# Attention with a bucketed bias, then a bilinear feed-forward: the bias loads, the order of the first four pairs, and where two feed-forward quanta and the fifth pair's transposes stand

## The chip, the cores and the metric

The kernel runs on one core of a Trainium2 chip. The metric is the time of one execution on the device in microseconds. Engines are named as in the profile: PE (TensorE's matmuls) with PEld (its weight loads), DVE (VectorE), ACT (ScalarE), POOL (GpSimd) and SP (SyncE), which here only issues DMAs. POOL issues DMAs too, and ACT can.

## The reference

Two stages. The first is attention over 8 batches and 8 heads with 576 positions and a head size of 64, with a bias that depends only on the distance of two positions, by 32 buckets:

```python
scores = scale * np.matmul(q, k.transpose(0, 1, 3, 2))
...
bias = bias_table[bucket]
scores = scores + bias.transpose(2, 0, 1)[None, :, :, :]
scores = scores - np.max(scores, axis=-1, keepdims=True)
attn = np.exp(scores)
attn = attn / (np.sum(attn, axis=-1, keepdims=True) + 1e-09)
return np.matmul(attn, v).astype(np.float32)
```

The second takes the result as x, 4608 tokens of 512, and computes `((x @ w_a) * (x @ w_b)) @ w_out` with an inner size of 1536. Inputs and output are float32; the kernel computes in bfloat16 with float32 sums.

## The kernel before

**Units of work.** Attention is done in 32 pairs, a pair being two heads of one batch; four pairs make a batch. A pair needs q and k transposed (head dimension on the partitions, tile `qkT`), six score tiles, each followed by an exponential on ACT (four wide ones of 128x1024 elements, two smaller ones, "scores rest"), multiplications with the band on DVE, ten "av" groups on PE that multiply with v and with a column of ones, and the division on DVE (`rc`, then `xg`). `emit_x` transposes the result into `xn`, the input of the feed-forward: in batch 0 on PE with a DVE copy, later by a DMA. The feed-forward is cut into 9 chunks of 512 tokens, each of 12 blocks. A block is two *quanta*: `pa` (four matmuls of 512 columns with w_a, then a copy `ha` on ACT) and `pb` (four with w_b, then the product `g` on DVE). After the blocks, `po` multiplies with w_out.

**The band.** All distances over 128 fall in the last bucket, so exp(bias) differs from a constant only near the diagonal; the constant cancels in the division. `emit_table` loads the 32-row table four times one under the other (`bt`), its last row on all partitions (`bl`), and a constant one-hot matrix (`oh`), takes the difference, its exponential, and makes `ebd`. `emit_band(k)`, k from 0 to 5, makes a sixth of the band with 16 small matmuls into one PSUM bank, which DVE copies to `E` (L189). `copy_band_tail` makes a shifted copy `Et` for the last score tile, on POOL (L197); pairs from the fifth on use it, while the first four do that multiplication in two halves of 64 partitions (L297).

**Order.** The schedule is written out by hand: each engine does its instructions in the order in which the Python code emits them. The first four pairs (batch 0) have a loop of their own, without feed-forward work beside them. In it the av groups of one pair stand among the scores of the next. After it come the last pair's av groups, its x, two quanta, the fifth pair's transposes (L237, `emit_transposes_first(4, ring=True)`), and two more quanta. From the fifth pair on, a pair is 9 steps and a quantum stands in most of them.

**PSUM.** Of eight banks, four serve the scores in turn (two tiles of two banks, pool `pst`), and four (`m0` to `m3`) are given out in turn by `bank`: two for "av" (band, warm matmuls, av groups, x) and two for "ffn" (transposes, later the quanta). After the first four pairs av has one bank and ffn three. A matmul into a bank waits until the reader of the bank's earlier content is done.

**Queues.** POOL issues the loads of q, k, v and the weights in one queue, and each load waits there for the eighth load before it to land. `set_v` are the memsets of v's tile (a column of ones, and zeros in the last block of rows), also on POOL. SP issues the bias loads and, much later, the stores and the transposing DMAs. `emit_warm(n)` issues n matmuls of zeros with 512 columns.

Of the kernel before, what the change touches and what calls it, by code (L numbers as in the profile page):

```python
# [13 lines left out]
def kernel(  # L14
# [11 lines left out]
    nc = tc.nc  # L26
# [8 lines left out]
    NB = 32  # L35
# [133 lines left out]
    def emit_table():  # L169
        for g in range(4):  # L170
            nc.sync.dma_start(out=bt_sb[32 * g:32 * g + 32, :], in_=bias_table)
        nc.sync.dma_start(out=bl_sb[:, :],
                          in_=bias_table[NB - 1:NB, :].to_broadcast([128, H]))
        nc.sync.dma_start(out=oh_sb[:, :], in_=oh_handle.ap())
        nc.vector.tensor_tensor(out=bt_sb[:, :], in0=bt_sb[:, :], in1=bl_sb[:, :], op=SUB)
        nc.scalar.activation(out=eb_sb[:, :], in_=bt_sb[:, :], func=ACTF.Exp)
        nc.vector.tensor_tensor(
            out=ebd_sb[:, :, :],
            in0=eb_sb[:, :].rearrange("b (a h) -> b a h", a=1).to_broadcast([128, 4, H]),
            in1=oh_sb[:, 512:544].rearrange("b (a h) -> b a h", a=4), op=MULT)  # L180

    def emit_band(k):

        ps = bank("av", [128, 64, H], FP32, f"E{k}")
        for j in range(16):
            s = 380 - 4 * (16 * k + j)
            nc.tensor.matmul(out=ps[:, 4 * j:4 * j + 4, :], lhsT=oh_sb[:, s:s + 128],  # L187
                             rhs=ebd_sb[:, :, :], start=True, stop=True)
        nc.vector.tensor_copy(out=E_sb[:, :, 64 * k:64 * k + 64],  # L189
                              in_=ps[:, :, :].rearrange("p c h -> p h c"))  # L190

    def copy_band_tail():

        for hh in range(2):

            r, c0 = slice(64 * hh, 64 * hh + 64), 64 * hh
            nc.gpsimd.tensor_copy(out=Et_sb[r, :, :], in_=E_sb[r, hh::2, c0:c0 + 192])  # L197
# [9 lines left out]
    def emit_transposes(p):  # L207
# [7 lines left out]
        ps = pst.tile([128, 2, 1024], BF16, tag="st", name=f"tr{p}")  # L215
        for which in range(2):
            for j in range(LJ):
                nc.tensor.transpose(ps[:, which, LP * j:LP * j + LP],
                                    qk_tiles[b][2][:, hp, which, j, :], ident[0:LP, 0:LP])
        nc.scalar.activation(  # L220
# [3 lines left out]
    def emit_transposes_first(p, k_act=False, ring=False):  # L224
# [5 lines left out]
        for which, t in enumerate(qk_tiles[b][0:2]):  # L230
# [17 lines left out]
            else:  # L248
                nc.vector.tensor_copy(out=o, in_=i)

# [85 lines left out]
    def emit_x(p):  # L336
# [9 lines left out]
        for jq in range(5):  # L346
            nc.tensor.transpose(ps[:, jq, :], xg_of[p][:, jq, :], ident[:, :])
        nc.vector.tensor_copy(out=xn[:, hp, S * b:S * b + S],  # L348
                              in_=ps[:, :, :].rearrange("p j t -> p (j t)")[:, 0:S])
# [5 lines left out]
    def ffn_quanta(c):  # L355
        g = wrk.tile([128, NDF, 512], BF16, tag="g", name=f"g{c}")
        for df in range(NDF):
# [28 lines left out]
    def all_quanta():  # L386
        for c in range(NCH):
            yield from ffn_quanta(c)

    quanta = all_quanta()  # L390


# [25 lines left out]
    set_v(0, nc.gpsimd)  # L418
    load_v(0, 0, 4)
    load_v_tail(0)  # L420
    load_qk(0, 4, 8)
# [3 lines left out]

    emit_transposes_first(0)
    emit_band(0)
    emit_tails(0)

# [5 lines left out]
    for p in range(4):  # L435
# [8 lines left out]
        else:  # L444
            emit_band(1)
            emit_band(2)
        emit_scores(p, 2)
        if p:
            emit_avs(p - 1, 0 if p == 1 else 4, 4 if p == 1 else 6)
        else:  # L450
            emit_band(3)
            emit_band(4)
        emit_scores(p, 3)
        if p < 3:
            emit_transposes_first(p + 1, k_act=(p == 1))
        if p:
            emit_avs(p - 1, 4 if p == 1 else 6, 10)
        else:
            emit_band(5)
# [3 lines left out]
        emit_scores_rest(p)  # L463
        if p == 0:
# [4 lines left out]
            copy_band_tail()  # L469
# [7 lines left out]
    emit_x(2)  # L477
    emit_avs(3, 0, 10)
    emit_x(3)
    banks.update(av=(0,), ffn=(2, 3, 1))  # L480
    next(quanta)
    next(quanta)
    emit_transposes_first(4, ring=True)
# [16 lines left out]
    for p in range(4, NP + 1):  # L500
# [7 lines left out]
        for s in range(9):  # L508
# [19 lines left out]
            if s == (4 if p == 5 else 1) and p + 1 < P_DMA:  # L528
                emit_transposes(p + 1)
# [62 lines left out]
```

## Time and profile before

| | us |
|---|---|
| median of 3 runs (419.4, 419.59, 420.15) | 419.59 |
| the profiled execution | 420.81 |
| its span, from the first to the last instruction | 419.0 |
| busy PE / DVE / ACT / POOL | 404.1 / 238.1 / 230.8 / 80.6 |
| first band matmul starts | 8.50 |
| first wide exponential starts | 9.82 |
| first scores of the second, third, fourth, fifth pair start | 15.70 / 21.53 / 26.86 / 40.71 |

Times inside a profile count from the span's start. The time of a run is longer than the span by what lies before and after the instructions, 1.81 us in the profiled execution. A line of the profile names the line of the kernel, the engine, the operation, the tile written and the tiles read; "idle" is the time for which the engine stood before that instruction, with the event that ended it. "Pair 0" is the first pair and "pair 4" the fifth, as in the names of the tiles; words ("the fifth pair") count from one.

### The profile page before, as it was taken

What the parts mean: (1) busy time and instruction counts of PE and PEld (TensorE: products, weight loads), DVE (VectorE), ACT (ScalarE), POOL (GpSimd) and SP (SyncE); (2) the same over time, 40 slices, a digit from 0 to 9 for tenths busy, and PEclk for the clock granted to TensorE, in tenths of its full rate; (3) what the DMA queues carried; (4) which work ended last, traced back from release to release, by engine and by line L of the source; (5) the groups of instructions that cost most, each with busy time, mean ns of one, the idle gap of its engine ahead of it and who ended that gap; (6) DMA issues with size and microseconds to landing.
All of it is one profiled execution on the core that took longest, in us unless ns stands there. A gap on an engine that the chain in (4) does not pass through costs nothing.

```text
span 419.0 us, 8668 instructions
## 1 busy us (share of the span) xinstructions
PE 404.1 (96%) x3488; PEld 208.0 (50%) x3488; DVE 238.1 (57%) x574; ACT 230.8 (55%) x313; POOL 80.6 (19%) x138
## 2 busy tenths in 40 slices
PE   5979999999999999999999999999999999999996
PEld 2655455545555555555555555454554554444442
DVE  3896666666565755576556656665546553332431
ACT  2993888556655666466646674567556631321320
POOL 8874531113111211103011311130000000000000
PEclk8899999999999999999999999999999999999999
DMA  9999994689759685968698978983242012002002
GB/s 97 159 208 188 200 140 57 138 173 182 104 94 207 115 100 109 199 107 125 97 167 150 131 102 148 180 126 53 70 119 45 17 40 94 1 2 100 2 0 100
DMA packets 109449, 46.60 MB, mean 111 GB/s; under 512 B 84576, under 2 KB 104800, under 8 KB 109408
## 3 DMA queue, kind: packets, MB, share of 16 engines
q0 software_dynamic: 54304, 18.88, 40.6%
q1 hardware_dynamic: 55104, 27.16, 26.4%
q8 instruction: 27, 0.44, 0.4%
q14 instruction: 14, 0.11, 0.1%
HBM read 37.90 MB, written 15.93 MB: 128 GB/s over the span
## 4 chain that ended last, share of the span: by engine, by line
PE 87%; DMA 3%; DVE 3%; ACT 3%; issue 1%; SPq 1%; DVEq 0%; ACTq 0%
PE pb L368 22%; PE pa L360 22%; PE po L377 21%; PE av L322 8%; PE st L266 7%; PE av L319 2%; ACT at L268 2%; DMA qk_scratch<-qkn 2%; PE st L284 2%; PE st L276 2%; DMA oh_sb<-oh_const 1%; DVE at L302 1%; DMA xn<-xg 1%; PE E L187 1%; DVE xg L332 1%
## 5 line engine op out<-in xcount | busy, mean ns | idle before, releaser
L268 ACT ACTIVATE at<-st 128x1024 bf16<-128x1024 f32 x128 | 123.9, 1022 | 51.5 <-PE st L266 50.9
L371 DVE TENSOR_TENSOR g<-pb,ha 128x512 bf16<-128x512 f32 x108 | 74.6, 691 | 76.2 <-PE pb L368 52.2
L364 ACT ACTIVATE ha<-pa 128x512 f32<-128x512 f32 x108 | 64.7, 599 | 92.8 <-PE pa L360 92.8
L360 PE MATMUL pa<-xn,wa 128*128 128x512 bf16 x432 | 111.2, 379 | 0.5 <-DMA xn<-xg 0.5
L368 PE MATMUL pb<-xn,wb 128*128 128x512 bf16 x432 | 111.0, 379 | 0.0
L377 PE MATMUL po<-wo,g 128*128 128x512 bf16 x432 | 101.7, 379 | 0.0
L322 PE MATMUL av<-vb,at 128*128 128x65 bf16 x1280 | 64.4, 194 | 0.0
L302 DVE TENSOR_TENSOR at<-at,E 128x768 bf16<-128x768 bf16 (+2 forms) x128 | 61.6, 501 | 4.6 <-ACT at L268 3.7
L377 PEld LDWEIGHTS <-g 128*128 128x128 bf16 x432 | 39.6, 98 | 49.0 <-issue 7.9
L322 PEld LDWEIGHTS <-at 128*128 128x128 bf16 x1280 | 55.4, 98 | 16.3 <-issue 1.5
L368 PEld LDWEIGHTS <-wb 128*128 128x128 bf16 x432 | 38.7, 97 | 46.4 <-issue 7.8
L360 PEld LDWEIGHTS <-wa 128*128 128x128 bf16 x432 | 38.5, 98 | 43.2 <-issue 7.0
L381 DVE COPY ob<-po 128x512 f32<-128x512 f32 x36 | 24.9, 692 | 52.5 <-PE po L377 52.4
L266 PE MATMUL st<-qkT 64*128 64x512 bf16 x256 | 41.3, 389 | 2.9 <-ACT at L279 1.2
L498 POOL COPY pace<-at 1x1 bf16<-1x1 bf16 x22 | 4.2, 192 | 179.4 <-DVE at L302 179.4
L319 PE MATMUL av<-vb,at 128*128 128x130 bf16 x160 | 35.5, 222 | 2.0 <-DVE xn L348 1.5
L332 DVE TENSOR_TENSOR xg<-av,rc 128x384 bf16<-128x384 f32 x64 | 31.4, 491 | 2.2
L279 ACT ACTIVATE at<-st 128x512 bf16<-128x512 f32 x32 | 19.2, 599 | 23.1 <-PE st L276 23.1
L133 POOL DMA_DIRECT2D vb<-in_v_dram x36 | 30.7, 864 | 5.9 <-PE pb L368 2.5
L330 DVE RECIPROCAL rc<-av 128x6 f32<-128x6 f32 x64 | 11.8, 185 | 27.8 <-PE av L322 27.8
L319 PEld LDWEIGHTS <-at 128*128 128x128 bf16 x160 | 15.6, 98 | 16.9 <-issue 2.3
L286 ACT ACTIVATE at<-st 128x576 bf16<-128x576 f32 x32 | 20.7, 647 | 0.0
(53 smaller groups left out, 184.4 us busy)
## 6 DMA issues: line engine op xcount, KB each, us to landing
out_dram<-ob SPq DMA_DIRECT2D x36, 256.0 KB, 2.4
qk_scratch<-qkn SPq DMA_DIRECT2D x22, 288.0 KB, 3.8
ql<-in_q_dram POOLq DMA_DIRECT2D x15, 288.0 KB, 5.5
kl<-in_k_dram POOLq DMA_DIRECT2D x15, 288.0 KB, 6.5
vb<-in_v_dram POOLq DMA_DIRECT2D x28, 128.0 KB, 6.4
wa<-in_moe_w_a_dram POOLq DMA_DIRECT2D x4, 384.0 KB, 10.2
wb<-in_moe_w_b_dram POOLq DMA_DIRECT2D x4, 384.0 KB, 11.0
wo<-in_moe_w_out_dram POOLq DMA_DIRECT2D x4, 384.0 KB, 8.0
```

The source lines that it names most:

```text
L133: nc.gpsimd.dma_start(out=vb2[b % 2][:, h0:h1, i, 0:Dh], in_=v[b, h0:h1, 128 * i:128 * i + 128, :].transpose([1, 0, 2]))
L266: nc.tensor.matmul(out=st[:, hh, :], lhsT=kT[r, 128 * i:128 * i + 128], rhs=qT[r, 0:512], start=True, stop=True)
L268: nc.scalar.activation(out=at[:, 2 * i:2 * i + 2, 0:512], in_=st[:, :, :], func=ACTF.Exp, scale=scale)
L302: nc.vector.tensor_tensor(out=at[:, sl, q0:q0 + w], in0=at[:, sl, q0:q0 + w], in1=e, op=MULT)
L319: nc.tensor.matmul(out=pav[:, j, :, :], lhsT=at[:, 8, 128 * jq:128 * jq + 128], rhs=vb[:, 2 * hp:2 * hp + 2, 4, :], start=True, stop=False)
L322: nc.tensor.matmul(out=pav[:, j, hh, :], lhsT=at[:, 2 * i + hh, 128 * jq:128 * jq + 128], rhs=vb[:, 2 * hp + hh, i, :], start=False, stop= ...
L332: nc.vector.tensor_tensor(out=xo.rearrange("p j (h d) -> p j h d", h=2), in0=pav[:, :, :, 0:Dh], in1=rc[:, 0:n, :, :].to_broadcast([128, n ...
L360: nc.tensor.matmul(out=ps[:, :], lhsT=wa_sb[:, mc, 128 * df:128 * df + 128], rhs=xn[:, mc, 512 * c:512 * c + 512], start=(mc == 0), stop=( ...
L364: nc.scalar.activation(out=ha[:, :], in_=ps[:, :], func=ACTF.Copy)
L368: nc.tensor.matmul(out=ps[:, :], lhsT=wb_sb[:, mc, 128 * df:128 * df + 128], rhs=xn[:, mc, 512 * c:512 * c + 512], start=(mc == 0), stop=( ...
L371: nc.vector.tensor_tensor(out=g[:, df, :], in0=ps[:, :], in1=ha[:, :], op=MULT)
L377: nc.tensor.matmul(out=ps[:, :], lhsT=g[:, df, 128 * tt:128 * tt + 128], rhs=wo_sb[:, df, :], start=(df == 0), stop=(df == NDF - 1))
```

## The change

1. *Bias loads.* `bt` is loaded with one broadcasting DMA instead of four, and `bt` and `bl` are issued by ACT; SP only issues `oh`. A one-element Exp, on data that is there at once, stands ahead of the table's exponential on ACT.
2. *Start of pair 0.* Bands 0 and 1 come ahead of pair 0's transposes, and band 2 right behind them. The transposes go into four quarter tiles (two of them in the scores' banks), copied by ACT and DVE, two each. ACT copies band 1.
3. *First four pairs.* The other bands move up by one place; pair 0's av groups all come behind pair 2's transposes (six of them) and behind pair 1's last scores (four). Warm matmuls: six are added, in pairs 0 and 1.
4. *Tail of the band.* It is copied by ACT instead of POOL, after the fourth pair's scores.
5. *Hand-over.* x2 is copied by ACT. The first two quanta (block 0 of chunk 0) are cut into four parts by the four slices of x; parts 0 and 1 come ahead of the fourth pair's av groups, parts 2 and 3 behind its x. The fifth pair's transposes come ahead of the fourth pair's x.
6. *Pair 5* (the sixth): its transposes use two ffn banks instead of a score tile, and are copied by ACT (q) and DVE (k).
7. *POOL's queue.* v's first loads come ahead of the memsets of v's tile, which in the built program then wait for these loads to land, and the load of q and k for heads 4 to 7 is cut in two.

```diff
     def emit_table():
-        for g in range(4):
-            nc.sync.dma_start(out=bt_sb[32 * g:32 * g + 32, :], in_=bias_table)
-        nc.sync.dma_start(out=bl_sb[:, :],
-                          in_=bias_table[NB - 1:NB, :].to_broadcast([128, H]))
+        nc.scalar.dma_start(out=bt_sb[:, :], in_=bias_table.rearrange("(g b) h -> g b h", g=1)
+                            .to_broadcast([4, NB, H]))
+        nc.scalar.dma_start(out=bl_sb[:, :],
+                            in_=bias_table[NB - 1:NB, :].to_broadcast([128, H]))
         nc.sync.dma_start(out=oh_sb[:, :], in_=oh_handle.ap())
+        nc.scalar.activation(out=pace_sb[:, :], in_=warm[0:1, 0:1], func=ACTF.Exp)
...
-    def emit_band(k):
+    def emit_band(k, act=False):
...
+        if act:
+            nc.scalar.activation(out=o, in_=i, func=ACTF.Copy)
+        else:
+            nc.vector.tensor_copy(out=o, in_=i)
...
-            nc.gpsimd.tensor_copy(out=Et_sb[r, :, :], in_=E_sb[r, hh::2, c0:c0 + 192])
+            nc.scalar.activation(out=Et_sb[r, :, :], in_=E_sb[r, hh::2, c0:c0 + 192], func=ACTF.Copy)
...
-    def emit_transposes(p):
+    def emit_transposes(p, ring=True):
...
+            p_ = ps[:, which, :] if ring else bank("ffn", [128, 1024], BF16, f"tr{p}_{which}")[:, :]
...
+    def emit_transposes_pair0():
+
+        qkT = wrk.tile([128, 2, S], BF16, tag="qkT", bufs=3, name="qkT0")
+        qkT_of[0], qT_of[0], kT_of[0] = qkT, qkT[:, 0, :], qkT[:, 1, :]
+        for which, t in enumerate(qk_tiles[0][0:2]):
+            o = qkT[:, which, :].rearrange("c (p j) -> c p j", j=LJ)
+            for half in range(2):
+                if which == 0:
+                    ps = bank("ffn", [128, 3, LP], BF16, f"tr0_0_{half}")
+                else:
+                    ps = pst.tile([128, 3, LP], BF16, tag="st", name=f"tr0_1_{half}")
+                for j in range(3):
+                    for hh in range(2):
+                        c0 = Dh * (3 * half + j)
+                        nc.tensor.transpose(ps[64 * hh:64 * hh + 64, j, :], t[:, hh, c0:c0 + Dh],
+                                            ident[0:LP, 0:LP])
+                o_ = o[:, :, 3 * half:3 * half + 3]
+                i_ = ps[:, :, :].rearrange("c j p -> c p j")
+                if half == 0:
+                    nc.scalar.activation(out=o_, in_=i_, func=ACTF.Copy)
+                else:
+                    nc.vector.tensor_copy(out=o_, in_=i_)
...
+    class EarlyQuanta:
+
+
+        def __init__(self):
+            self.g = wrk.tile([128, NDF, 512], BF16, tag="g", name="g0")
+            self.ps = [ffn_bank(f"{n}0_0") for n in ("pa", "pb")]
+
+        def part(self, mc):
+            for ps, w_sb in zip(self.ps, (wa_sb, wb_sb)):
+                nc.tensor.matmul(out=ps[:, :], lhsT=w_sb[:, mc, 0:128], rhs=xn[:, mc, 0:512],
+                                 start=(mc == 0), stop=(mc == NMC - 1))
+            if mc == NMC - 1:
+                ha = wrk.tile([128, 512], FP32, tag="ha", name="ha0_0")
+                nc.scalar.activation(out=ha[:, :], in_=self.ps[0][:, :], func=ACTF.Copy)
+                nc.vector.tensor_tensor(out=self.g[:, 0, :], in0=self.ps[1][:, :], in1=ha[:, :],
+                                        op=MULT)
...
     load_qk(0, 2, 4)
-    set_v(0, nc.gpsimd)
     load_v(0, 0, 4)
     load_v_tail(0)
-    load_qk(0, 4, 8)
+    set_v(0, nc.gpsimd)
+    load_qk(0, 4, 6)
+    load_qk(0, 6, 8)
     load_v(0, 4, 8)
     load_w_in(0)
     load_qk(1, 0, 4)
 
-    emit_transposes_first(0)
     emit_band(0)
+    emit_band(1, act=True)
+    emit_transposes_pair0()
+    emit_band(2)
     emit_tails(0)
...
         else:
-            emit_band(1)
-            emit_band(2)
-        emit_scores(p, 2)
-        if p:
-            emit_avs(p - 1, 0 if p == 1 else 4, 4 if p == 1 else 6)
-        else:
             emit_band(3)
             emit_band(4)
+        emit_scores(p, 2)
+        if p > 1:
+            emit_avs(p - 1, 4, 6)
+        elif p:
+            emit_warm(3)
+        else:
+            emit_band(5)
+            emit_warm(1)
         emit_scores(p, 3)
         if p < 3:
             emit_transposes_first(p + 1, k_act=(p == 1))
         if p:
-            emit_avs(p - 1, 4 if p == 1 else 6, 10)
+            emit_avs(p - 1, 0 if p == 1 else 6, 6 if p == 1 else 10)
         else:
-            emit_band(5)
+            emit_warm(2)
             emit_mult(0, 0)
             emit_mult(0, 1)
         emit_mult(p, 2)
         emit_scores_rest(p)
+        if p == 1:
+            emit_avs(0, 6, 10)
...
-            copy_band_tail()
...
-    emit_x(2)
+    emit_x(2, act=True)
+    copy_band_tail()
+    early = EarlyQuanta()
+    early.part(0)
+    early.part(1)
     emit_avs(3, 0, 10)
+    emit_transposes_first(4, ring=True)
     emit_x(3)
+    early.part(2)
+    early.part(3)
+    quanta = all_quanta(early)
     banks.update(av=(0,), ffn=(2, 3, 1))
-    next(quanta)
-    next(quanta)
-    emit_transposes_first(4, ring=True)
     emit_tails(4)
...
-                emit_transposes(p + 1)
+                emit_transposes(p + 1, ring=(p > 4))
```

## The prediction

> **What bounds the kernel now.** I read the page, then the busy time by stage, then the timeline of the first 45 us, then the waits. The page first:
>
> ```profile
> PE 404.1 (96%) x3488; PEld 208.0 (50%) x3488; DVE 238.1 (57%) x574; ACT 230.8 (55%) x313; POOL 80.6 (19%) x138
> PEclk8899999999999999999999999999999999999999
> ```
>
> TensorE is the bound over the whole, but not everywhere. The stages (start:end, length, then busy us and count of PE, PEld, DVE, ACT, POOL, granted clock, DMA share, GB/s):
>
> ```profile
> 8.20:14.80 6.60, 6.22 (x132) 4.36 (x133) 4.97 (x10) 4.46 (x5) 6.60 (x10) 0.55 1.33 122
> 16.10:22.00 5.90, 4.37 (x83) 2.98 (x83) 5.34 (x16) 5.90 (x10) 4.47 (x7) 1.00 1.41 195
> 22.00:27.30 5.30, 4.68 (x88) 3.31 (x88) 4.61 (x15) 5.30 (x9) 3.00 (x8) 1.00 1.22 206
> 27.30:33.60 6.30, 4.17 (x67) 3.01 (x66) 5.96 (x14) 4.92 (x7) 4.63 (x7) 1.00 1.18 209
> 41.00:60.00 19.00, 18.29 (x158) 9.09 (x155) 12.86 (x31) 16.37 (x22) 8.19 (x13) 1.00 1.36 180
> 90.00:300.00 210.00, 210.00 (x1805) 107.80 (x1804) 127.85 (x323) 128.54 (x174) 37.80 (x63) 1.00 0.79 130
> ```
>
> From 41 us on PE never stops for long (two waits, 0.57 and 0.45 us), so whatever brings the fifth pair's first scores (40.71) forward shortens the run one for one. Before that ACT is full from 16.10 to 27.30, and PE has spare time. The places where it is lost, from the timeline (start, length, engine, line; in brackets the idle time before and what ended it):
>
> ```profile
> 3.06 0.43 SPq L174 DMA_DIRECT2D oh_sb<-oh_const  x1
> 8.50 0.59 PE L187 MATMUL E<-ebd_sb,oh_sb 128*128 128x32 bf16 x16 [2.55 <-DVE ebd_sb L177]
> 9.82 2.96 ACT L268 ACTIVATE at<-st 128x1024 bf16<-128x1024 f32 x3 [2.51 <-PE st L266]
> 27.40 1.79 POOL L197 COPY Et<-E 64x768 bf16<-64x768 bf16 x2
> 27.55 1.76 DVE L297 TENSOR_TENSOR at<-at,E 64x192 bf16<-64x192 bf16 x2
> 31.38 0.22 PE L319 MATMUL av<-vb,at 128*128 128x130 bf16 x1 [1.51 <-DVE xn L348]
> 32.48 0.60 ACT L279 ACTIVATE at<-st 128x512 bf16<-128x512 f32 x1 [1.38 <-PE st L276]
> 33.68 0.23 PE L319 MATMUL av<-vb,at 128*128 128x130 bf16 x1 [0.49 <-ACT at L286]
> 44.65 0.39 PE L266 MATMUL st<-qkT 64*128 64x512 bf16 x2 [0.57 <-ACT qkT L220]
> ```
>
> The bias table holds up the first band, and through DVE's queue the first scores; the first exponential starts at 9.82 and ACT is the bound until about 31. There the POOL copy of the band's tail slows DVE, PE waits 1.51 us for a bank that DVE must empty, and ACT 1.38 us for PE.
>
> **Step 1, the bias loads.** SP issued four table quarters (0.41 us each), `bl` at 2.60 and `oh` at 3.06. Now `oh` is SP's first, at about 0.75, and ACT issues `bt` and `bl` at about 0.75 and 1.17. `bl` took 3.6 us to land, the `bt` quarters 1.5 to 2.8; I take 2.8 (the loads of q and k move 180 GB/s only from 3.5 us on), so it is there at 4.0. `oh` took 5.1 us beside those loads; an output store of 256 KB takes 2.4, so I take 3.2 us as its landing. From `bl` to the first band matmul lie 0.17 + 0.21 + 0.19 us of work and hand-offs, 0.7: **4.8 us** instead of 8.50. Ends: 4.0 (the six warm matmuls end at 3.94) and 6.2 (`oh` keeps its 5.1). ACT's table load (1.28) and the new one-element Exp end near 3.1, hidden by `bl`.
>
> A page of the Trainium skill, "DMA: Bandwidth & Descriptors", section "Issuing engines are not separate DMA queues", speaks against this step: a second issuing queue saves only issue time, since all share the same DMA engines. By it the landings keep their length, the band starts at 6.2 and the sum below loses 1.4 us. "ScalarE: Activation LUTs", section "What ACT_TABLE_LOAD costs", has 1.38 us of drain besides the 1.28: ACT would be free at 4.5, and 0.3 us is lost; in this trace the next ACTIVATE starts 0.32 us after the load's end, itself waiting for DVE.
>
> **Step 2, the start of pair 0.** Two bands now stand ahead of pair 0's 24 transposes and one behind them. Sixteen band matmuls took 0.41 to 0.59: 0.9 for two, 5.7. The transposes take 0.63 (24.46 to 25.09), 6.35; the third band 0.45, 6.8. ACT copies band 1 (0.60, as other 128x512 forms) and two quarters of q and k (0.42 each, from 1.02 at 1024 and 0.60 at 512 elements), to 7.15; DVE band 0 (0.69) and two quarters (0.45 each, from 0.75 for twice that), to 6.95. The scores start at 7.2 instead of 9.17, the first exponential, 0.65 later, at 7.85: **2.0 us early**.
>
> **Step 3, ACT's chain through three pairs.** ACT does the same work from there on, so it keeps its lead unless it starves. In pair 0 it had gaps of 0.52 and 0.19. Before the fourth exponential PE has, at the half clock of that stage, 1.03 + 0.97 + 0.54 + 0.50 + 0.43 + 0.54 = 4.0 us from 7.2, so 11.3, where ACT is ready at 10.8: a gap of 0.5 as before. The warm matmuls added in pairs 0 and 1 (six, 0.22 to 0.43 us each) lie in PE's spare time (1.5 of 5.9 us). Pair 0's av groups now all stand behind pair 2's transposes: DVE idles some 2 us there and then has `rc` and `xg` twice and three multiplies in a row, 0.20 + 0.56 + 0.17 + 0.42 + 0.55 + 0.50 + 0.52 = 2.9, from 18.5 (when these av groups are through) to 21.4. Behind it, without a gap, stand `bd` 0.39, two multiplies 1.0, x0's copy 0.45, `rc` and `xg` 0.76 and the copy of pair 3's k, 0.75: it ends at 24.75 instead of 26.22, just when ACT is through with pair 2. The first exponential of pair 3 falls to 25.45 from 27.29: **1.85**.
>
> **Step 4, the band's tail on ACT.** DVE's two half multiplies go back from 0.88 to 0.26 each and the copies after them from 0.70 to 0.39: 1.55 us off the queue that x1's bank waits for. The bank is free at about 28.7 (was 31.33), the last av groups of pair 2 take 0.62, and pair 3's next scores are there at 29.6, with ACT free at 29.25: of its 1.38 us gap 0.45 stay, and pair 3's last exponential ends at 30.9 (was 33.63). **0.85 more.** The tail copies (two of 64x768, 0.82 each) and x2's (0.65) run on ACT behind that, to 33.2, where ACT had stood idle from 33.63 to 37.49; the fifth pair's copy, next in ACT's queue, comes at 33.6, so they cost nothing. If that cover went, it would delay this copy and `ha` behind it.
>
> **Step 5, the hand-over.** From pair 3's last exponential to the fifth pair's scores it took 33.63 to 40.71, 7.08 us. Now half of the first two quanta fills the wait for the last multiply (done 0.5 after it), av of pair 3 takes 1.55, the transposes 0.63 in the place of the wait for `xg`, x 0.45, part 2 0.40, part 3 0.45 after 0.15 of waiting for x's copy, the next quanta 0.90 and 0.85. `pb` of the second block must take the bank of the first: 0.60 for `ha` and 0.70 for the product stand before it, a new wait of 0.45. Sum 6.3: **0.8 more**.
>
> **Step 6, pair 5's transposes in the feed-forward banks.** The 0.57 us wait at 44.65 goes. In its place `pb` of block 2 finds its turn in the bank of its own `pa`, and waits for `ha`, which is queued behind two exponentials: 2.92 us after the first scores instead of 2.02. The scores behind it then wait for nothing, and block 3 starts at 4.3 instead of 4.26 us: a cost of 0.1 at most.
>
> **Step 7, POOL's queue.** v's loads stand ahead of the memsets of v's tile, and these wait for all six to land. The last is issued at 8.14; landing took 2.5 at least and 5.0 in the middle; with 2.5 and 1.13 of memsets the third pair's q and k go out at 12.0 instead of 9.93, in two parts (one issue of 0.7 more each). They land 3.4 to 4.4 us later, at 16.1 to 17.1; ACT wants them by 17.4. The fifth pair's k had landed 19.7 us after that point (16.7 until the weights' first half at 26.6, and 0.59 MB at 200 GB/s): 31.7, wanted at 32.9. Both hidden, the second by 1.2 us. SP loses five issues that nothing else waits for.
>
> **Sum.** 1.85 + 0.85 + 0.8 - 0.1 = 3.4 us. The profiled execution took 420.81 us (span 419.0), 1.22 above the median; from it 417.4, and by the median 419.59 - 3.4 = **416.2**.
>
> **Rivals.** (a) The loads take over: with 5.0 us of landing, POOL's memsets end at 14.3, the third pair's k lands at 18.4 to 19.4 and the fifth pair's at 34.0; some 1.5 us go, 417.7. For it: DMA moves about 200 GB/s all through. Against: v's loads fall into the slack at 10.5 to 12.5, where 36 to 71 GB/s moved. (b) The clock: it was 0.50 from 7.25 to 14.05 and opened after a stretch with PE full. If PE, with its bands done, is not full enough, pair 1 (4.4 us of PE work in 5.9) runs at half speed too and costs about 1.4: 417.6. (c) The bias comes no sooner, because ACT's queue starts late or slowly: the band stays at 8.5 and only steps 4 and 5 are left, 418.1. (d) The other sign: v's tails land so late that the third pair's transposes stop PE and ACT. Past 17.4 every us counts; at 20.8, a tail landing of 7.1 us, the 3.4 are gone, and at 9 us it is 421.5. For it: the 128 KB loads of v took 11.7 in full traffic; against: the small ones 4.9 and 5.0.
>
> **How the numbers follow.** What I forecast, a gain of 2.0 to 4.6 (step 1's ends take 1.35 off or add 0.8, a full clock in pair 0 0.4 more): 0.66; (a) 0.12, (b) 0.08, (c) 0.04, (d) 0.10. The range goes from 415.0 to 418.4, a gain of 1.2, below (a) to (c); left out are (d) and the outer edges, under 0.2. A difference of 0.2% (0.84 us) is what can be told from none. Slower takes 0.08 of (d); the rest of it and an edge of (a) make 0.04 for the same; faster is 0.88.
>
> **What would show it.** Step 1: the first band matmul near 4.8. 2: the first wide ACT exponential near 7.85. 3: pair 3's first near 25.5. 4: no half multiply of 0.88 on DVE, and no wait of 1.5 for x1's copy. 5: the fifth pair's scores near 37.3, with waits on `g`. 6: a wait of 0.8 on `ha` in block 2. Wrong would be a PE wait on ql or kl before the third or fifth pair's transposes (a, d), or a clock of 0.5 past 14 us (b).

## The result and the profile after

| | before | after |
|---|---|---|
| median, us (5 runs each) | 419.40 | 417.84 |
| lowest and highest | 419.10 to 420.15 | 417.36 to 417.85 |
| the profiled execution | 420.81 | 417.62 |
| its span | 419.0 | 415.9 |

The ratio is 0.9957, with an interval of 0.9943 to 0.9972. It compares the means (417.70 and 419.50 us): by it the changed kernel is faster by 0.43%, or 1.80 us. The medians differ by 1.56 us. Both are about half of the 3.4 us that were forecast. The two profiled executions differ by 3.19 us. A later comparison gave the changed kernel 417.82 (12 runs) beside 419.43 for the kernel before (22 runs).

The front of the profiled execution of the changed kernel, from the timeline (start, length, engine, line; in brackets the idle time before and what ended it):

```profile
0.75 0.35 SPq L174 DMA_DIRECT2D oh_sb<-oh_const  x1
0.75 1.14 ACTq L170 DMA_DIRECT2D bt_sb<-in_bias_table_dram  x1
1.93 0.34 ACTq L172 DMA_DIRECT2D bl_sb<-in_bias_table_dram  x1
5.35 0.17 DVE L176 TENSOR_TENSOR bt_sb<-bt_sb,bl_sb 128x8 f32<-128x8 f32 x1 [2.71 <-DMA bl_sb<-in_bias_table_dram]
6.04 1.01 PE L188 MATMUL E<-ebd_sb,oh_sb 128*128 128x32 bf16 x32 [2.09 <-DVE ebd_sb L178]
6.98 0.69 PE L280 MATMUL tr<-ident,ql 96*64 96x96 bf16 x12
9.47 2.85 ACT L306 ACTIVATE at<-st 128x1024 bf16<-128x1024 f32 x3 [1.02 <-PE st L304]
10.69 0.39 PE L304 MATMUL st<-qkT 64*128 64x512 bf16 x2
12.48 1.02 ACT L306 ACTIVATE at<-st 128x1024 bf16<-128x1024 f32 x1 [0.15 <-PE st L304]
```

The bias still holds up the first band, 2.46 us less than before (6.04 against 8.50), and since the transposes now stand behind two bands, PE idles for 2.09 us. The first wide exponential comes only 0.35 us earlier than the 9.82 of before. The twelve transposes take 0.69 us, where the same twelve take 0.45 from 12.37 on: PE runs at about half its rate until some point before 10.69, where two score matmuls take 0.39 as they do later.

The same view for the hand-over from the fourth to the fifth pair, and one wait behind it:

```profile
26.17 3.82 ACT L306 ACTIVATE at<-st 128x1024 bf16<-128x1024 f32 x4
26.43 0.51 DVE L335 TENSOR_TENSOR at<-at,E 64x192 bf16<-64x192 bf16 x2
29.12 0.22 PE L357 MATMUL av<-vb,at 128*128 128x130 bf16 x1 [0.37 <-DVE xn L390]
30.23 0.60 ACT L317 ACTIVATE at<-st 128x512 bf16<-128x512 f32 x1 [0.24 <-PE st L314]
31.79 1.69 ACT L201 ACTIVATE Et<-E 64x768 bf16<-64x768 bf16 x2
36.78 1.02 PE L426 MATMUL pb<-xn,wb 128*128 128x512 bf16 x4 [0.33 <-DVE g L410]
37.74 0.60 PE L304 MATMUL st<-qkT 64*128 64x512 bf16 x4
40.65 1.02 PE L426 MATMUL pb<-xn,wb 128*128 128x512 bf16 x4 [0.82 <-ACT ha L422]
48.25 0.22 PE L357 MATMUL av<-vb,at 128*128 128x130 bf16 x1 [0.50 <-DMA vb<-in_v_dram]
```

DVE's two half multiplications take 0.51 us (1.76 before), PE's wait for x1's bank is 0.37 (1.51), the last small exponentials' gap 0.24 (1.38). The fifth pair's scores start at 37.74 (40.71). New is the last line: PE waits for the second batch's v.

The chain of waits for the first 48 us, followed back from that wait (start, length, what), shows what this v stood behind:

```profile
8.06 2.65 DMA vb<-in_v_dram
10.76 0.24 POOL vb L89
...
17.94 7.47 DMA wb<-in_moe_w_b_dram
25.41 0.28 issue
25.69 14.10 DMA wb<-in_moe_w_b_dram
39.80 0.02 issue
39.82 0.02 POOLq L139
39.84 0.49 issue
40.33 7.79 DMA vb<-in_v_dram
```

Apart from the landings it is POOL's queue from end to end: v's first loads, the memsets behind them, then the weights, then the second batch's v.

### The profile page after: what moved, and what is told of

The parts are those of the page before. It is cut to its first block, busy times and chain, and to the rows that moved or that the text cites. A ratio compares the mean times of both kernels' runs of the same rounds, so it can differ in the third digit from the quotient of the medians.

```text
span 415.9 us, 8678 instructions
## 1 busy us (share of the span) xinstructions
PE 404.5 (97%) x3494; PEld 208.7 (50%) x3494; DVE 237.0 (57%) x574; ACT 233.3 (56%) x319; POOL 80.3 (19%) x138
## 4 chain that ended last, share of the span: by engine, by line
PE 87%; DMA 8%; POOL 3%; issue 1%; ACT 1%; DVE 0%; POOLq 0%
PE po L435 23%; PE pb L426 22%; PE pa L418 21%; PE av L360 8%; PE st L304 7%; DMA wb<-in_moe_w_b_dram 5%; DMA vb<-in_v_dram 3%; PE av L357 2%; PE st L322 2%; POOL vb L133 1%; PE st L314 1%; POOL kl L112 1%; POOL ql L112 1%; PE tr L224 0%; ACT at L306 0%
## 5 line engine op out<-in xcount | busy, mean ns | idle before, releaser
L418 PE MATMUL pa<-xn,wa 128*128 128x512 bf16 x428 | 110.0, 379 | 0.0
L133 POOL DMA_DIRECT2D vb<-in_v_dram x36 | 30.7, 861 | 7.8 <-PE pb L426 2.5
```

The costliest lines, as they stand in the source:

```text
L133: nc.gpsimd.dma_start(out=vb2[b % 2][:, h0:h1, i, 0:Dh], in_=v[b, h0:h1, 128 * i:128 * i + 128, :].transpose([1, 0, 2]))
L418: nc.tensor.matmul(out=ps[:, :], lhsT=wa_sb[:, mc, 128 * df:128 * df + 128], rhs=xn[:, mc, 512 * c:512 * c + 512], start=(mc == 0), stop=( ...
```

## The experiments

Every kernel below computes the whole reference. Stages are compared in each kernel's profiled execution, in us; "rest" is the span from the fifth pair's first scores to the end:

| kernel | first band | first wide exponential | pair 1's first | pair 3's first | fifth pair's scores | rest | median |
|---|---|---|---|---|---|---|---|
| before | 8.50 | 9.82 | 16.13 | 27.29 | 40.71 | 378.3 | 419.40 |
| before, again | 8.21 | 9.53 | 15.95 | 27.10 | 40.30 | 377.7 | 419.8 (one run) |
| step 1 alone | 6.86 | 8.44 | 14.22 | 25.66 | 37.95 | 377.4 | 418.52 |
| step 4's copy alone | 8.14 | 9.57 | 15.35 | 26.51 | 38.80 | 377.7 | 418.26 |
| after | 6.04 | 9.47 | 15.01 | 26.17 | 37.74 | 378.2 | 417.84 |
| after, again | 6.03 | 9.47 | 15.48 | 26.64 | 38.21 | 377.5 | 417.82 |
| memsets first | 6.14 | 9.58 | 15.27 | 26.44 | 38.01 | 377.5 | 417.33 |
| transposes first | 7.17 | 8.55 | 14.95 | 26.10 | 37.67 | 377.7 | 417.74 |
| bias on SP | 5.40 | 8.84 | 15.00 | 26.28 | 38.48 | 379.4 | 419.39 |
| step 6 undone | 6.11 | 9.54 | 15.40 | 26.55 | 38.13 | 377.4 | 417.60 |
| no added warm matmuls | 6.26 | 9.45 | 14.74 | 27.01 | 38.58 | 377.4 | 417.61 |
| steps 6, 7 undone | 6.17 | 9.61 | 15.73 | 26.89 | 38.46 | 377.3 | 417.57 |
| the same, `bl` first on SP | 5.05 | 8.49 | 13.93 | 25.08 | 36.65 | 377.4 | 415.86 |
| step 1 undone | 8.44 | 11.87 | 17.85 | 29.01 | 40.58 | 378.9 | 420.08 |

The kernel before stood beside them three times, with medians of 419.21 (first four experiments), 419.72 (the next four) and 419.43 (the last four); its runs spread over 2.2 to 3.2 us within one comparison, so a single profiled execution says little about differences under 1 us. The three comparisons were made on three chips. Where a median is set against the 417.84 of the changed kernel from another comparison, differences of about 0.5 us are not told apart: the kernel before moved by as much between the comparisons. The ratios are each taken to the kernel before of the same comparison, and they follow the means more than the medians.

**The kernel before, once more** (no edit).

> The kernel before, unchanged, to see how far one profiled execution of it stands from another. Theory: the prediction's sum was made on an execution of 420.81 us, 1.4 above the median of its kernel; another execution near 419.4 differs in the stretch before the fifth pair's first scores (40.71) or in the 0.45 us that PE waited for the transposing DMA near 89 us, and so part of the 3.1 us between the two profiled spans is not the change's. Rival: all executions of the kernel before have the same inner times (first wide exponential 9.82, fifth pair's scores 40.71) and differ only outside the span.

It took 419.8 us, span 418.0, 1.0 less than the first profiled execution. Of this, 0.41 was gained by the fifth pair's scores and the rest behind them; the wait of 0.45 for `xn` that the first execution had is absent. The place where the band's tail is copied, from the timeline:

```profile
27.36 0.51 DVE L297 TENSOR_TENSOR at<-at,E 64x192 bf16<-64x192 bf16 x2
28.33 1.80 POOL L197 COPY Et<-E 64x768 bf16<-64x768 bf16 x2
28.51 2.03 DVE L302 TENSOR_TENSOR at<-at,E 128x512 bf16<-128x512 bf16 x2
30.96 0.22 PE L319 MATMUL av<-vb,at 128*128 128x130 bf16 x1 [1.28 <-DVE xn L348]
```

The half multiplications of L297, which the first execution showed slowed, run at full speed here, because POOL came to its copy 0.9 us later. The copy then slows the next multiplications (L302: 2.03 for two, which took 0.89 in the first execution, where the copy was over by then), and PE waits 1.28 us instead of 1.51. The collision's place moves with POOL's queue, the price stays near.

**Step 1 alone, on the kernel before:**

```diff
-        for g in range(4):
-            nc.sync.dma_start(out=bt_sb[32 * g:32 * g + 32, :], in_=bias_table)
-        nc.sync.dma_start(out=bl_sb[:, :], ...
+        nc.scalar.dma_start(out=bt_sb[:, :], in_=bias_table ... .to_broadcast([4, NB, H]))
+        nc.scalar.dma_start(out=bl_sb[:, :], ...
+        nc.scalar.activation(out=pace_sb[:, :], in_=warm[0:1, 0:1], func=ACTF.Exp)
```

> The kernel before with the bias loads of the change and nothing else. Theory: the first band matmul starts near 6.0 instead of 8.5 as in the changed kernel, DVE comes to its copy of k right behind, the first scores start near 6.9 instead of 9.17, earlier than the 8.82 of the changed kernel, and ACT's chain keeps some 1 to 2 us of it: 417.5 to 418.5. Rival: the bands, at half clock, starve ACT in pair 0 and the lead is lost there: 419.2 or more.

Median 418.52, at the upper end of what was expected, ratio 0.9976 (0.9960 to 0.9992). One of the 12 runs took 2305.45 us; why is not known, and the ratio leaves it out. The profiled execution was one of the fastest, 417.12. The band started at 6.86 and not near 6.0, because in the old order k's transposes stand ahead of it and k landed late:

```profile
6.49 0.45 PE L238 MATMUL tr<-ident,kl 96*64 96x96 bf16 x12 [0.87 <-DMA kl<-in_k_dram]
```

But only one band stands between these transposes and the scores, so the first exponential started at 8.44, a full us ahead of the changed kernel. And the hand-over shows what happens when POOL's copy falls elsewhere:

```profile
25.92 0.51 DVE L298 TENSOR_TENSOR at<-at,E 64x192 bf16<-64x192 bf16 x2
28.40 1.70 POOL L198 COPY Et<-E 64x768 bf16<-64x768 bf16 x2
28.61 0.22 PE L320 MATMUL av<-vb,at 128*128 128x130 bf16 x1 [0.37 <-DVE xn L349]
```

POOL still copies the tail, but DVE is through with the band multiplications that the copy had slowed: beside the copy it does `rc` and `xg`, which read PSUM and take their usual 0.19 and 0.56 us. The wait for x1's bank is 0.37, as in the changed kernel. From pair 3's first exponential to the end of its last one it took 5.20 us here, 6.34 and 6.11 in the two executions of the kernel before, 5.21 in the changed one. An earlier front thus took away by itself what step 4 was to take away: in this execution the two gains were not additive.

**Step 4's copy alone, on the kernel before:** the tail is copied on ACT behind the fourth pair's scores.

```diff
-            nc.gpsimd.tensor_copy(out=Et_sb[r, :, :], in_=E_sb[r, hh::2, c0:c0 + 192])
+            nc.scalar.activation(out=Et_sb[r, :, :], in_=E_sb[r, hh::2, c0:c0 + 192], func=ACTF.Copy)
```

> The kernel before with the band's tail copied by ACT behind the fourth pair's scores, and nothing else. Theory: DVE's two half multiplies take 0.26 instead of 0.88 us, PE's wait of 1.51 us for x1's bank shrinks to about 0.3, and the run is 1.0 to 1.2 us shorter: 418.3. Rival: ACT or the loads hold up the same place and at most 0.3 us are gained: 419.1 or more.

Median 418.26, 0.95 below the median of the kernel before beside it, ratio 0.9989 (0.9973 to 1.0005), so not told from no change by the interval: nine of the 12 runs lie at 418.14 to 418.58, three at 419.84 to 420.05. The profiled execution has the wait for x1's bank at 0.37, the 5.21 us through pair 3, and 7.08 us from there to the fifth pair's scores, exactly as in the kernel before: pair 3 became 0.9 to 1.1 us shorter, and the ACT copies cost nothing; DVE's two half multiplications took 0.52 beside them. The rest of this execution's lead is no work of the edit: pair 3's first exponential, ahead of anything that was changed, already came 0.78 us sooner than in the first execution of the kernel before.

**Memsets first:** the changed kernel with v's memsets ahead of v's loads again.

```diff
+    set_v(0, nc.gpsimd)
     load_v(0, 0, 4)
     load_v_tail(0)
-    set_v(0, nc.gpsimd)
```

> The changed kernel with v's memsets ahead of v's first loads again, as before the change. Theory (loads): the memsets' wait leaves the DMA engines empty from 10.5 to 13 us, some 0.5 MB at 200 GB/s, and every later load is late by 2 us; without it the fifth pair's av groups no longer wait for v (0.50 us), and the time falls by 0.5 to 0.7 us against the changed kernel, to about 417.2. Rival: the hole is filled later and the wait only moves to another place: the same time, 417.8.

Median 417.33, ratio 0.9953 (0.9937 to 0.9970). The stretch 10.5 to 13.0 in the busy time by stage, first the changed kernel, then this one (start:end, length, busy us and count of PE, PEld, DVE, ACT, POOL, granted clock, DMA share, GB/s):

```profile
10.50:13.00 2.50, 2.39 (x56) 1.48 (x53) 1.88 (x3) 2.35 (x3) 2.11 (x7) 1.00 0.00 0
```

```profile
10.50:13.00 2.50, 2.50 (x56) 1.45 (x54) 1.98 (x3) 2.31 (x4) 2.50 (x5) 1.00 1.01 104
```

In the changed kernel the DMA engines move nothing for 2.5 us, because POOL waits 2.02 us for v and all later loads stand behind it. With the memsets first the hole is gone, and so is the wait of 0.50 for v at 48.25. By the medians it is worth 0.5 us, by the ratios (0.9953 and 0.9957) 0.2, and the two intervals do not separate it from nothing.

**Transposes first:** the first pair's transposes ahead of every band, one band ahead of its scores, the others behind them.

```diff
-    emit_band(0)
-    emit_band(1, act=True)
     emit_transposes_pair0()
-    emit_band(2)
+    emit_band(0)
     emit_tails(0)
...
-            emit_band(3)
-            emit_band(4)
+            emit_band(1)
+            emit_band(2)
         emit_scores(p, 2)
```

> The changed kernel with the first pair's transposes ahead of every band, one band ahead of its scores, and the other five behind the scores, two by two. Theory (step 2's lead was lost to the order: TensorE stood 2.1 us behind the bands with q landed, and then ran at half its rate): the transposes run from about 4.8 to 6.5 us, the first wide exponential starts near 8.1 instead of 9.47, pair 3's first exponential near 25.0 instead of 26.17, and the time is about 416.7 (417.84 with the change). Rival (scalar engine's lead is eaten again by the five bands between the scores and by DVE, which has to copy them all): first exponential near 8.1, but pair 1's first near 15.0 as with the change, and the time 417.5 to 418.5.

From the timeline of this kernel:

```profile
5.31 0.69 PE L280 MATMUL tr<-ident,ql 96*64 96x96 bf16 x12 [1.36 <-DMA ql<-in_q_dram]
6.55 0.69 PE L280 MATMUL tr<-ident,kl 96*64 96x96 bf16 x12 [0.55 <-DMA kl<-in_k_dram]
8.55 2.96 ACT L306 ACTIVATE at<-st 128x1024 bf16<-128x1024 f32 x3 [1.01 <-PE st L304]
11.93 0.69 PE L252 MATMUL tr<-ident,ql 96*64 96x96 bf16 x12
12.04 1.02 ACT L306 ACTIVATE at<-st 128x1024 bf16<-128x1024 f32 x1 [0.52 <-PE st L304]
```

The rival's numbers came out, but not only its reason. The first exponential is 0.92 us earlier, but pair 1's is at 14.95 against 15.01, with a gap of 0.52 before the fourth exponential instead of 0.15. The bands between the scores, and DVE's copies of all six, are one reason. Another is PE's rate: twelve transposes still take 0.69 us at 11.93, where the changed kernel was at full rate by 10.69; this execution does not tell the two apart. The median is 417.74 (ratio 0.9943, 0.9922 to 0.9965), the same as with the change. q and k land at about 5.3 and 6.5 us, and the last of the bias at 5.5, so neither order wins.

**Bias on SP:** the changed kernel with the queues of the bias exchanged.

```diff
-        nc.scalar.dma_start(out=bt_sb ...)
-        nc.scalar.dma_start(out=bl_sb ...)
-        nc.sync.dma_start(out=oh_sb[:, :], in_=oh_handle.ap())
+        nc.sync.dma_start(out=bl_sb ...)
+        nc.sync.dma_start(out=bt_sb ...)
+        nc.scalar.dma_start(out=oh_sb[:, :], in_=oh_handle.ap())
```

> The changed kernel with the two bias loads on SP, ahead, and the one-hot table on the scalar engine's queue. Theory (step 1 missed because the scalar engine's first DMA issue took 1.14 us, and bl stood behind it): bl leaves at 0.75 instead of 1.93 and lands 3.3 us later, near 4.1; the first band matmul starts near 4.9 instead of 6.04, the first wide exponential near 8.4 instead of 9.47; time about 416.9. Rival (bl's landing is set by when the tiny loads are served beside q's and k's, not by its issue): bl lands near 5.2 again, the band stays at 6.0, and the time within 0.3 us of the 417.84 with the change.

```profile
0.75 0.36 ACTq L174 DMA_DIRECT2D oh_sb<-oh_const  x1
1.19 0.73 SPq L172 DMA_DIRECT2D bt_sb<-in_bias_table_dram  x1
12.69 0.24 POOL L89 MEMSET vb<- 128x32 bf16 x1 [3.93 <-DMA vb<-in_v_dram]
34.36 0.45 PE L252 MATMUL tr<-ident,kl 96*64 96x96 bf16 x12 [0.53 <-DMA kl<-in_k_dram]
49.75 0.22 PE L357 MATMUL av<-vb,at 128*128 128x130 bf16 x1 [1.26 <-DMA vb<-in_v_dram]
```

The cause that I had named fell: ACT's first DMA issue takes 0.36 us when it is `oh`, and the long issue goes with `bt`, the one load in four copies (1.14 on ACT, 0.73 on SP). The band came 0.64 us earlier, but the time was 419.39, 1.55 above the changed kernel. v landed late, POOL's memsets waited 3.93 us instead of 2.02, every later load left 1.9 us later, and PE then waited for the fifth pair's k, for the second batch's v and 0.4 us for `xn`. So the late landing of v that rival (d) feared did come, but the price, 1.55 for 1.9 us of delay, was paid at the places of rival (a): the third pair's transposes did not wait, the fifth pair's did. v was late in the run with step 1 undone (below) as well, which also has its bias loads on SP: the 32 KB loads of v took 4.2 us to land there, 4.8 here, and 2.8 in the changed kernel. Why it is late is not shown by these runs.

**Step 6 undone:** pair 5's transposes in the score ring again.

```diff
-                emit_transposes(p + 1, ring=(p > 4))
+                emit_transposes(p + 1)
```

> The changed kernel with step 6 alone undone: pair 5's transposes go through the score ring again. Theory (step 6 moves 0.1 us at most): the wait of 0.82 us on the first feed-forward copy in block 2 becomes 0.2 or less, the wait of 0.57 on the transposes' copy is back, and the time is within 0.3 us of the 417.84 with the change. Rival (the borrowed bank is a cost that the stage's 0.14 us hides): 0.4 us or more faster.

Median 417.60, 0.24 below the changed kernel; the wait of 0.82 on `ha` is gone, that of 0.57 on the transposes' copy is back. By the medians the step moves about 0.2 us, which no interval here can tell from nothing (ratio 0.9944, 0.9923 to 0.9964).

**No added warm matmuls:** the six in pairs 0 and 1 removed.

```diff
-        elif p:
-            emit_warm(3)
-        else:
+        elif p == 0:
             emit_band(5)
-            emit_warm(1)
         emit_scores(p, 3)
...
-            emit_warm(2)
             emit_mult(0, 0)
```

> The changed kernel without the six warm matmuls that it adds in the first two pairs. Theory (they lie in TensorE's spare time, and the clock would be open without them): granted clock 1.00 in each 5 us up to 30 us, time within 0.4 us of the 417.84 with the change. Rival (they are what keeps the clock open): a stretch of several us at 0.50 between 8 and 20 us, as in the kernel before, and 418.5 to 419.5, with runs that scatter by 1 us or more.

Median 417.61 (ratio 0.9941, 0.9919 to 0.9963), within the expected 0.4 us, but in the profiled execution the clock did not stay open. Busy time by stage, the granted clock in the third column from the right, first two rows of the changed kernel, then this one:

```profile
5.00:10.00 5.00, 3.83 (x84) 2.76 (x84) 2.99 (x8) 2.10 (x5) 3.74 (x6) 1.00 1.58 143
15.00:20.00 5.00, 4.30 (x80) 2.90 (x80) 3.33 (x11) 5.00 (x8) 5.00 (x8) 1.00 1.50 127
```

```profile
5.00:10.00 5.00, 3.61 (x84) 2.55 (x84) 2.99 (x8) 2.08 (x5) 3.75 (x6) 0.74 1.59 144
10.00:15.00 5.00, 4.14 (x86) 2.86 (x84) 4.23 (x8) 5.00 (x8) 4.07 (x10) 0.92 0.41 54
15.00:20.00 5.00, 3.91 (x63) 2.98 (x61) 2.47 (x9) 4.62 (x7) 5.00 (x8) 0.76 1.52 134
```

From 17.7 to 21.2 us the av groups ran at half rate, and pair 1 took 6.99 us from its first exponential to the next pair's instead of 5.83: 1.16 us, near the 1.4 of rival (b). It is made up where this execution waits less (pair 0 took 5.29 instead of 5.54, and nothing waits for v). So in this execution both readings had half of it. That the warm matmuls keep the clock open is not shown, though: the mean granted clock of this run is 0.992, that of the other five is 0.998 to 1.000, and 3.5 us at half rate would alone make 0.996. The half rate in pair 1 may be a matter of this one execution.

**The changed kernel again** (no edit).

> The changed kernel itself, unaltered, beside the others of this comparison. It should be at 417.4 to 418.0 again, with runs that lie within 0.6 us of each other.

Median 417.82, ratio 0.9975 (0.9962 to 0.9989), with runs up to 419.73, so wider than expected. The profiled execution, 417.44, has the same front to 9.47, but PE reached its full rate only after 12.3 us, so pair 0 took 6.01 instead of 5.54. PE does not wait for v: the engines were 0.47 us later at the fifth pair, which gave the loads the time. Which of the two comes last, the loads or the engines, is thus a matter of half a us.

**Steps 6 and 7 undone:** memsets first, `load_qk(0, 4, 8)` in one part, pair 5's transposes in the ring.

```diff
+    set_v(0, nc.gpsimd)
     load_v(0, 0, 4)
     load_v_tail(0)
-    set_v(0, nc.gpsimd)
-    load_qk(0, 4, 6)
-    load_qk(0, 6, 8)
+    load_qk(0, 4, 8)
...
-                emit_transposes(p + 1, ring=(p > 4))
+                emit_transposes(p + 1)
```

> The changed kernel with steps 6 and 7 undone: v's memsets ahead of v's loads, the third and fourth pairs' q and k in one part again, pair 5's transposes in the score ring. Theory (the loads' order costs 0.5 by POOL's wait for v, the split another 0.2 or so by 1.1 us of issuing, and step 6 up to 0.2): no wait of TensorE on vb near 48 us, DMA at 75 GB/s or more from 10.5 to 13.0, the fifth pair's first scores at 37.7 to 38.0 as with the change, and a time of 416.8 to 417.2. Rival (the fifth pair's lead is what counts, and the loads were hidden): within 0.3 us of the changed kernel beside it.

Median 417.57, ratio 0.9959 (0.9944 to 0.9973): 0.25 below the changed kernel beside it, where 0.6 to 1.0 was expected. By the medians the rival had it, and the loads are mostly hidden with the front where it is. By the means the difference is 0.69 (418.11 and 417.42), since three of the changed kernel's 12 runs took 418.8 to 419.7 and none of these five more than 417.69. The intervals overlap, so the size stays open between 0.25 and 0.7.

**The same with `bl` first on SP,** `oh` behind it, `bt` alone on ACT:

```diff
         nc.scalar.dma_start(out=bt_sb ...)
-        nc.scalar.dma_start(out=bl_sb ...)
+        nc.sync.dma_start(out=bl_sb ...)
         nc.sync.dma_start(out=oh_sb[:, :], in_=oh_handle.ap())
```

> As the run with steps 6 and 7 undone, and bl as the first load on SP, the one-hot table behind it, bt alone on the scalar engine's queue. Theory (the loss in the run with both bias loads on SP came through v's late landing and POOL's memsets behind it, which no longer wait): bl lands near 4.1, the first band matmul starts at 5.0 to 5.4, the first wide exponential at 8.4 to 8.8 and pair 3's first 0 to 0.7 us sooner than with the change, since TensorE's half rate decides in pair 0; 416.2 to 417.0. Rival (the two bias loads on SP cost by themselves, wherever POOL stands): slower by 1 us or more than the run beside it.

```profile
0.75 0.39 SPq L172 DMA_DIRECT2D bl_sb<-in_bias_table_dram  x1
4.36 0.17 DVE L176 TENSOR_TENSOR bt_sb<-bt_sb,bl_sb 128x8 f32<-128x8 f32 x1 [1.72 <-DMA bt_sb<-in_bias_table_dram]
5.05 1.02 PE L188 MATMUL E<-ebd_sb,oh_sb 128*128 128x32 bf16 x32 [1.10 <-DVE ebd_sb L178]
8.49 3.93 ACT L306 ACTIVATE at<-st 128x1024 bf16<-128x1024 f32 x4 [1.02 <-PE st L304]
9.60 0.39 PE L304 MATMUL st<-qkT 64*128 64x512 bf16 x2
```

Median 415.86, ratio 0.9928 (0.9911 to 0.9946), under the 416.2 to 417.0 expected: 1.7 us below the run with steps 6 and 7 undone, from which it differs in this line alone, and 2.0 below the changed kernel. Five of its six runs lie at 415.71 to 415.92, the sixth took 417.79. `bl` lands 2.6 us after its issue, and now `bt` is the last, at 4.36. The band starts 1.12 us earlier than in the run beside it; PE is at its full rate by 9.60, ACT has no gap in pair 0, and pair 0 takes 5.44 us instead of 6.12. The 1.12 of the band and the 0.68 of pair 0 make the 1.8 us by which the fifth pair's scores are earlier. No PE wait on a load is left: the loads, in the old order again, can serve the earlier front.

**Step 1 undone:** the six bias loads on SP, the rest as changed.

```diff
-        nc.scalar.dma_start(out=bt_sb ... .to_broadcast([4, NB, H]))
-        nc.scalar.dma_start(out=bl_sb ...)
+        for g in range(4):
+            nc.sync.dma_start(out=bt_sb[32 * g:32 * g + 32, :], in_=bias_table)
+        nc.sync.dma_start(out=bl_sb ...)
```

> The changed kernel with step 1 alone undone: the bias by six loads on SP, the last two bl and the one-hot table, while the bands still stand ahead of the first pair's transposes. Theory (the new order makes the bias the gate of everything, so step 1 is what the order lives on): first band matmul at 8.2 to 8.5, first scores 2.8 us behind it at 11.0 to 11.3, first wide exponential near 11.8, 2.3 us later than with the change, and 419.2 to 420.2. Rival (the front is covered by the loads behind it): 418.5 or less.

```profile
8.44 1.01 PE L188 MATMUL E<-ebd_sb,oh_sb 128*128 128x32 bf16 x32 [4.49 <-DVE ebd_sb L178]
11.87 2.96 ACT L306 ACTIVATE at<-st 128x1024 bf16<-128x1024 f32 x3 [1.02 <-PE st L304]
```

Median 420.08, as the theory had it: 2.26 above the changed kernel, and above the kernel before (ratio 1.0017, 1.0003 to 1.0031). With the bands ahead of the transposes, PE stands 4.49 us for the bias. Not all of the price need be the bias's own landing: POOL's memsets waited 3.30 us for v here, and in the profiled execution (421.23, 1.15 above the median) PE waited another 0.98 for `xn` at 90.42. Without step 1, then, steps 2 to 7 together are a loss, although steps 4 and 5 are among them.

## Why the prediction was right or wrong

The direction and the range held; the gain was 1.56 instead of 3.4. By its steps, in the profiled executions ("early" is the lead over the kernel before at that point, "more" what a step adds to it):

| | forecast | measured |
|---|---|---|
| 1: first band matmul | 4.8 | 6.04 |
| 2: first wide exponential | 7.85 (2.0 early) | 9.47 (0.35 early) |
| 3: pair 3's first exponential | 25.45 (1.85 early) | 26.17 (1.12 early) |
| 4: more by pair 3's last exponential | 0.85 | 1.13 |
| 5: more by the fifth pair's scores | 0.8 | 0.72 |
| 6: block 3 | -0.1 | -0.14 |
| 7: loads | hidden | 0.50 of wait at 48.25 |
| sum, profiled executions | 3.4 | 3.19 |
| sum, medians | 3.4 | 1.56 |

**Step 1** failed on `bl`. Its own terms, 4.0 and 0.7, make 4.7 and not 4.8, but that is not what it missed by. I had `bl` issued at 1.17 and landed 2.8 later. It was issued at 1.93, behind the 1.14 us issue of `bt`, and landed 3.3 to 3.4 later, nearly the old 3.6. `oh` was the better way round, 2.1 instead of 3.2. The rule that I set against the step (the Trainium skill, "DMA: Bandwidth & Descriptors", "Issuing engines are not separate DMA queues") gave a band at 6.2 by keeping the landings; the band came at 6.04, but for another reason: the landing that this 6.2 rested on, `oh`'s, did not keep its length but went from 5.1 to 2.1, and it was `bl` that came last. What `bl` cost is shown by the last but one experiment: issued first, it was there before `bt`, and the band came at 5.05.

**Step 2** failed on the rate of PE. I took the 24 transposes at 0.63, from a row at 24 us; here they took 1.10 (6.98 to 8.08), and the third band 0.61 instead of 0.45. The trace of the kernel before had a nearer row, the 24 transposes from 13.19 to 14.22 in the stage at half clock, 1.03; step 3 counted with that clock, step 2 did not. Band to scores was 2.78 us instead of 2.4. Transposes first would not have been better (417.74).

**Step 3** was better than forecast: 16.70 us from the first wide exponential to pair 3's first, instead of 17.6, because PE was at full rate by 10.69 and ACT's gap before the fourth exponential was 0.15, not 0.5. All of what was won lies in pair 0; pairs 1 and 2 took 11.16 us in both kernels. How much is a matter of the execution: 17.17 when the same kernel was profiled again.

**Steps 4, 5 and 6** were right in mechanism and near in size; the tail's copy alone showed step 4 to be the copy, though with step 1 alone the same 1.1 us came without it, so what step 4 adds in the changed kernel is not shown: no run has that kernel with the copy on POOL. The hand-over, 7.08 or 7.09 us in all four executions without step 5, became 6.36.

**Step 7** followed the loads of the third and the fifth pair, which were indeed hidden, and left out the second batch's v, at the far end of the same queue. The wait of 0.50 is there in one of the two executions of the changed kernel; it was absent with the memsets first.

**The sum** came out for the pair of profiled executions (417.4 forecast, 417.62 measured), but by luck. The rows of the steps add up to 2.33 (1.12 + 1.13 + 0.72 - 0.14 - 0.50). The other 0.86 belongs to no step: 0.45 is the wait for `xn` that this execution of the kernel before had, about 0.3 lies behind the last matmul, and 0.1 I cannot place. The same 3.4, taken off the median, failed. The profiled execution of before lay 1.41 us above its median and that of after 0.22 below: 3.19 - 1.41 - 0.22 = 1.56. Some of the excess is in the very places that the steps were priced from: the kernel before, profiled again, was 0.41 us earlier at the fifth pair's scores, and lacked 0.45 us of waiting behind them. Which places make up the rest of the 1.41 stays open, since the median execution itself was not profiled.

Rival (a), 417.7, is near the measured time but not the main cause: removing its mechanism gave 0.25 to 0.5 by the medians. (b) did not come in the changed kernel, whose rows stand at a clock of 1.00; the one profiled execution without the warm matmuls had it, at 1.16. (c) did not come: the band started 2.46 us sooner, and step 1 is worth 2.26 in the new order. (d) did not come either, but one exchange of queues brought v's late landing about.

## What to carry to other kernels

Price a change against several executions: a gain read in one profiled execution that lies above its median contains that excess, and a collision between engines can move or vanish when a queue shifts by 1 us. When a late input is made the first thing that a queue waits for, the order lives on that input, so look for the last of its loads and give that one the first issue; here 1.7 us were left in one line. With waiting memsets in POOL's queue, another exchange that also put `bl` first lost 1.55 us. So when waiting instructions enter a load queue, follow the queue to its end, not only to the next consumer.

## What the runs showed of the hardware

- One load that broadcasts a 32-row table four times took 1.14 to 1.16 us to issue on ACT and 0.73 on SP; `bl` and `oh` took 0.34 to 0.43 on either, and the quarters of `bt` 0.41 to 0.43 on SP.
- The granted clock in the profile's rows does not tell when PE begins at full rate. In the changed kernel it is 1.00 throughout, while twelve transposes take 0.69 us at 6.98 and 0.45 at 12.37. The full rate came at most 4.7 us behind the first band there and where `bl` was first, but over 6 us behind it when the changed kernel was profiled again. The Trainium skill, "TensorE: Matmul & The Clock Gate", "Part 1: The HAM clock gate", has a free-running window of 3.4 us that decides this, so that the point varies by 0.5 us either way with where the first matmul falls in it. That the point varies agrees; the scatter here, from at most 4.7 to over 6 us, is larger, and the window itself is not seen in any run.
- Without the warm matmuls a half rate returned at 17.7 us in the profiled execution, behind 3.5 us with PE busy for 1.85 (13.5 to 17.0); in the changed kernel PE was busy for 2.70 there, and it did not. A busy share alone does not tell: in the kernel before, 2.13 of 3.4 us (30.7 to 34.1) left the clock at 1.00.
- POOL's copies of the tail (two of 64x768 elements) slowed the band multiplications that DVE did beside them by 1.1 to 1.3 us in two executions of the kernel before. In the run of step 1 alone, `rc` and `xg`, which read PSUM, kept their times beside the same copies. Beside ACT's copies, in the run of step 4's copy alone, two half multiplications with the band took their usual 0.52 us.
